# A guard of two columns becomes two guards of one column, a hand-written order of 745 operations replaces one of 725, and some casts change engine

## The chip, the cores and the metric

The kernel runs on one core of one Trainium2 chip. The metric is the device time of one execution in microseconds (us). Three runs of the kernel before gave 1259.17, 1256.1 and 1259.45 us; the median is 1259.17. The core's engines work side by side and wait for one another by semaphores: TensorE (PE, matrix products), VectorE (DVE), ScalarE (ACT), GpSimd (POOL) and SyncE (SP), whose queue here issues nearly all DMAs. Each engine carries out its own instructions in the order in which they were written.

## The reference, cut to what matters

An attention layer over 12288 tokens of 128 channels, with 768 keys made by pooling and one product, and then two feed-forward layers of width 2048:

```python
kv_pool = kv.reshape(B, H // r, r, W // r, r, C).mean(axis=(2, 4))
k = v = kv_pool.reshape(B, -1, C) @ w_sr
a = softmax(scale * (q @ k.T))
x = a @ v
h = x @ w_in
y = (maximum(h, 0) + alpha * minimum(h, 0)) @ w_out
h2 = y @ w_in2
out = (h2 * sigmoid(1.702 * h2)) @ w_out2
```

All inputs are float32 except the feed-forward weights, which come as 64-bit floats.

## The kernel before, in words

**Precision.** Nearly every product of float32 matrices is made as three float16 matmuls: each operand is split into a scaled high part and the rest (hi and lo), and hi·hi, lo·hi and hi·lo are summed in PSUM (`mm3`; lines 443 to 445 of the profile). Each split needs a power-of-two scale, which comes from the largest absolute value of the operand: `top_of` reduces each partition to its largest value (DVE), `total` (line 622) sums these over the partitions with a one-column matmul against a matrix of ones (called "scmm" here), and small DVE operations make the scale of the sum.

**The guard.** For tiles j > 2 the reduced values are raised to at least 2**-60 before `total`: one small DVE instruction, `max(a, 2**-60)`, called the guard. `x_prep(j)` prepares the attention's output x of tile j for the first feed-forward layer; for 2 < j < 22 it also prepares q of tile j+2, and there the two columns (column 0: x, column 1: q) go through one guard of 128x2, one scmm and one mask `scp`. In the profile the guard is `td<-ta` at line 408 (a helper's line), the scmm is `<-td,ones` at line 622.

**Tiles.** The tokens are cut into 24 tiles of 512. Of each tile there are four attention subtiles of 128 tokens (`att_tile`: product S, row maximum on DVE, exponential `exp` on ACT, normalised high part `ah` on ACT, low part `al` on DVE, and two DMA transposes `eh` and `el` issued by SP), six products with v (`att_v`), and 16 steps each of four feed-forward products: `l1`, `l2` with w1 and w2, `l3`, `l4` with w3 and w4. One step of l1 and of l3 needs two ACT operations (activation and high part), one DVE operation and a low part, mostly on POOL.

**Where the exponential goes.** For tiles 0 and 1 `exp` writes into an SBUF buffer `e` (two of them); for later tiles it writes back into PSUM, over S. The table `LO_ACT` says for which subtiles the low part is made on POOL, after a second scaled copy `es` on ACT.

**The start.** Twelve blocks of kv (512 KB each), q0 and q1 (256 KB each) and the eight weight blocks (1 MB each, "raw") are loaded over SP's queue. The pooled keys are twelve `kvmm` products; five of the blocks are first folded on DVE or POOL (`kvred`, table `KV_ON`). The weights are turned from 64-bit floats to pairs of float16 on chip (`conv`: per half matrix some 5 or 6 operations of 0.7 to 2.4 us on ACT, DVE and POOL; tables `CONV`, `HI_VEC`, `LO_VEC` choose the engine) after a reduction that finds their scale (`stats`).

**The order of the work.** `record` lists 6453 operations with a cost each, and `Plan.order` lays them out: first the operations whose numbers stand in the list `ORDER`, in that order (725 of them, up to about the second tile), then greedily by priority: at each step every engine's earliest ready operation is looked at, with the ends and latencies that the planner reckons. An operand may carry an offset, `(buffer, part, off)`: the planner then reckons it ready `off` ns earlier (a negative one: later). Offsets and costs change the order alone; the program's own waits are made by semaphores. Instructions are written in the order of the planned starts. [...] In gaps that the planner sees on PE between 20 and 60 us it puts dummy matmuls ("warm", line 1072).

What the steps below touch: `total` (616), `scale_of` (629), `att_tile` (around 686), `x_prep` (757), the tables from 323 on, and `ORDER` (86).

Of the kernel before, what the change touches and what calls it, by code (L numbers as in the profile page):

```python
# [16 lines left out]
AF = mybir.ActivationFunctionType  # L17
ALU = mybir.AluOpType
# [52 lines left out]
class Op:  # L71
# [14 lines left out]
ORDER = [3, 7, 8, 15, 9, 11, 10, 17, 16, 23, 13, 14, 20, 12, 18, 47, 171, 1, 2, 48, 49, 172, 41, 25, 26, 173, 4, 42, 27, 174, 50, 51, 175, 44, 52,  # L86
# [238 lines left out]
LO_ACT = [[1, 0, 1, 0], [0, 0, 0, 0]]  # L325
VEC = {'g1h': [0, 8384, 41304], 'g1l': [256, 128, 11032], 'g2h': [2560, 33322, 58609], 'g2l': [40298, 8194, 2884]}
GPS = {'g1': [0, 32896, 16], 'g2': [2688, 2, 20480]}
CONV = {'w10': 3, 'w11': 2, 'w20': 3, 'w21': 2, 'w30': 1, 'w31': 1, 'w40': 2, 'w41': 3}
LO_VEC = {'w10': 0, 'w11': 0, 'w20': 0, 'w21': 0, 'w30': 0, 'w31': 0, 'w40': 0, 'w41': 1}
HI_VEC = {'w10': 1, 'w11': 2, 'w20': 0, 'w21': 1, 'w30': 1, 'w31': 0, 'w40': 0, 'w41': 0}  # L330
# [53 lines left out]
def record(nc, T):  # L384

    pl = Plan()
    op = pl.op
# [11 lines left out]
    A = None if nc is None else nc.scalar  # L399
    G = None if nc is None else nc.gpsimd  # L400
# [11 lines left out]
    def small(fn, r, w, prio, gate=None, occ=66, dur=150, name="small", lock=False):  # L412
        return op("DVE", occ, dur, fn, r, w, prio, gate, name, lock)
# [22 lines left out]
    def new(name):  # L436
        return rings[name].buf(name)
# [178 lines left out]
    def total(pool, cols_, least, prio, n=1):  # L616

        pm = pool.buf("pt")

        def f():  # L620
            for i, (c, _) in enumerate(cols_):
                mm(out=pm.ap[:, 0:n], lhsT=T["ones"], rhs=c(), start=i == 0, stop=least is None and i == len(cols_) - 1)  # L622
            if least is not None:
                mm(out=pm.ap[:, 0:n], lhsT=T["ones"], rhs=least, start=False, stop=True)
        op("PE", 45 * len(cols_) + (45 if least is not None else 0), 0, f, [b for _, b in cols_] + [B["ones"]], [pm], prio, name="scmm")
        return pm

    def scale_of(d, pool, kc, kcb, prio, j=0):
        if j > 2:
            a, d = d, new("td")  # L630
            small(lambda: ts(d.ap, a.ap, 2.0 ** -60, ALU.max), [a], [d], prio)
        pm = total(pool, [(lambda: d.ap, d)], None if j > 2 else T["least"], prio)
# [48 lines left out]
    def att_tile(j, t, prio, gate):  # L681
# [23 lines left out]
        e = new("e") if j < 2 else s  # L705
        sm = new("sm")
        src = lambda: s.ap[:, :, 0:HALF]
        dst = (lambda: e.ap) if j < 2 else src
# [7 lines left out]
        op("ACT", 800, 905, lambda: A.activation(ah.ap, dst(), AF.Copy, scale=r.ap), [e, r], [ah], prio + 1.6, name=f"ah{j},{t}")  # L716
# [5 lines left out]
        if j < 2 and LO_ACT[j][t]:  # L722
# [7 lines left out]
        else:  # L730
            op("DVE", 933, 1019, lambda: V.scalar_tensor_tensor(out=al.ap, in0=dst(), scalar=r.ap, in1=ah.ap, op0=ALU.mult,  # L731
                                                                op1=ALU.subtract), [e, r, ah], [al], prio + 2.2, name=f"al{j},{t}",
               lock=j < 2)
# [25 lines left out]
    def x_prep(j, prio):  # L759
        x = xacc[j]  # L760
        pl.tag = f"X{j}"
        if 2 < j < NB - 2:
# [5 lines left out]
            small(lambda: ts(d.ap, a.ap, 2.0 ** -60, ALU.max), [(a, 0), (a, 1)], [d], prio + .01)  # L768
            pm = total(pool_h, [(lambda: d.ap, d)], None, prio + .1, 2)
# [346 lines left out]
```

## Time and profile before

| | us |
|---|---|
| median of three runs (lowest, highest) | 1259.17 (1256.1, 1259.45) |
| the profiled execution's own time | 1257.87 |
| its span in the trace | 1255.8 |
| PE busy in the span | 1215.5 (97%) |
| ACT busy | 1099.7 (88%) |
| DVE busy | 1005.0 (80%) |
| POOL busy | 804.8 (64%) |

The span is what the trace shows from the first instruction to the last; 2.1 us lie around it. "Busy" counts an engine's instructions, the dummy matmuls among PE's. Matmuls overlap: one of 512 columns is listed with 379 ns, and in a row of them the next starts after 215 ns.

### The profile page before, as it was taken

To read this page: it belongs to the slowest core of one execution; us is meant where nothing else is said; L and a number is where in the kernel's file an instruction comes from. 1 tells how busy PE (TensorE), PEld (TensorE's weight loads), DVE (VectorE), ACT (ScalarE), POOL (GpSimd) and SP (SyncE) were. 2 spreads that over 40 slices of the span, in tenths; PEclk is the share of its full clock that TensorE was granted. 3 is DMA by queue.
4 is the path that set the end of the run, shared out by engine and by line. 5 is a ranking of instruction groups with operands and counts; after the bars stand their busy time and mean duration, and the time that the engine had idled before them with its cause. 6 is when DMAs were issued, how large, how long until landed. Compare 5 with 4: busy or idle time off the path is not lost.

```text
span 1255.8 us, 18308 instructions
## 1 busy us (share of the span) xinstructions
PE 1215.5 (97%) x5829; PEld 569.3 (45%) x5832; DVE 1005.0 (80%) x1821; ACT 1099.7 (88%) x1939; POOL 804.8 (64%) x688
## 2 busy tenths in 40 slices
PE   5699999999999999999999999999999999999998
PEld 4344444444444444444444444444444444444443
DVE  5999998887877877878778778787787787876756
ACT  1899888888989989889899898898998988988888
POOL 1577566666657666666576666665766766667764
PEclk9999999999999999999999999999999999999999
DMA  9932222222121123121211221212111212120000
GB/s 372 215 62 48 44 43 47 53 37 46 35 55 35 36 45 55 34 47 34 56 34 38 43 55 34 46 36 55 34 40 41 55 34 47 34 47 13 9 10 17
DMA packets 165377, 66.67 MB, mean 53 GB/s; under 512 B 156448, under 2 KB 156576, under 8 KB 164256
## 3 DMA queue, kind: packets, MB, share of 16 engines
q1 hardware_dynamic: 164992, 65.43, 23.4%
q8 instruction: 45, 0.74, 0.2%
q14 instruction: 52, 0.43, 0.1%
q10 hardware_dynamic: 288, 0.07, 0.0%
HBM read 21.05 MB, written 6.29 MB: 22 GB/s over the span
## 4 chain that ended last, share of the span: by engine, by line
PE 60%; DVE 3%; ACT 1%; issue 0%; DMA 0%; POOLq 0%; POOL 0%; SPq 0%; ACTq 0%
PE bk L445 12%; PE bk L444 12%; PE bk L443 12%; PE hb L443 6%; PE hb L444 6%; PE hb L445 6%; PE sa L692 1%; PE sa L693 1%; PE sa L696 1%; DVE td L408 1%; DVE arena L832 1%; DVE ta L766 1%; ACT arena L808 0%; DMA q<-in_q 0%; PE hb L622 0%
## 5 line engine op out<-in xcount | busy, mean ns | idle before, releaser
L811 POOL TENSOR_TENSOR arena<-arena 128x512 f16<-128x512 f32 x656 | 769.0, 1191 | 403.4 <-ACT arena L808 286.9
L808 ACT CAST arena<-arena 128x512 f16<-128x512 f32 x740 | 449.5, 631 | 64.4 <-DVE arena L832 27.1
L873 DVE SCALAR_TENSOR_TENSOR arena<-arena,hb 128x512 f32<-128x512 f32 x261 | 178.8, 685 | 57.6 <-ACT arena L871 55.2
L832 DVE SCALAR_TENSOR_TENSOR arena<-arena,oma,hb 128x512 f32<-128x512 f32 x262 | 194.4, 743 | 29.9 <-ACT arena L830 26.3
L871 ACT ACTIVATE arena<-hb,yu 128x512 f32<-128x512 f32 x261 | 183.1, 702 | 12.8 <-PE hb L445 11.2
L830 ACT ACTIVATE arena<-hb 128x512 f32<-128x512 f32 x262 | 160.3, 613 | 23.1 <-PE hb L445 18.3
L445 PE MATMUL bk<-arena,w2h 128*128 128x512 f16 x384 | 145.6, 379 | 0.7 <-POOL arena L811 0.7
L445 PE MATMUL bk<-arena,w4h 128*128 128x512 f16 x384 | 145.6, 379 | 0.2 <-POOL arena L811 0.2
L444 PE MATMUL bk<-arena,w4l 128*128 128x512 f16 x384 | 145.6, 379 | 0.0
L443 PE MATMUL bk<-arena,w4h 128*128 128x512 f16 x384 | 145.6, 379 | 0.0
L444 PE MATMUL bk<-arena,w2l 128*128 128x512 f16 x384 | 145.6, 379 | 0.0
L443 PE MATMUL bk<-arena,w2h 128*128 128x512 f16 x384 | 145.6, 379 | 0.0
L873 DVE SCALAR_TENSOR_TENSOR arena<-arena,bk 128x512 f32<-128x512 f32 x123 | 84.1, 683 | 37.4 <-ACT arena L871 37.1
L731 DVE SCALAR_TENSOR_TENSOR alo<-sa,r,ah 128x768 f16<-128x768 f32 x88 | 89.5, 1017 | 18.1 <-ACT ah L716 13.0
L832 DVE SCALAR_TENSOR_TENSOR arena<-arena,oma,bk 128x512 f32<-128x512 f32 x122 | 90.7, 744 | 12.6 <-ACT arena L830 10.0
L443 PE MATMUL hb<-xh,w1h 128*128 128x512 f16 x262 | 99.2, 379 | 1.2 <-ACT xh L640 0.9
L443 PE MATMUL hb<-yh,w3h 128*128 128x512 f16 x261 | 98.9, 379 | 0.8 <-DVE arena L873 0.8
L445 PE MATMUL hb<-xl,w1h 128*128 128x512 f16 x262 | 99.3, 379 | 0.2 <-DVE xl L642 0.2
L444 PE MATMUL hb<-xh,w1l 128*128 128x512 f16 x262 | 99.3, 379 | 0.0
L445 PE MATMUL hb<-yl,w3h 128*128 128x512 f16 x261 | 98.9, 379 | 0.0
L444 PE MATMUL hb<-yh,w3l 128*128 128x512 f16 x261 | 98.9, 379 | 0.0
L871 ACT ACTIVATE arena<-bk,yu 128x512 f32<-128x512 f32 x123 | 85.3, 693 | 12.2 <-PE bk L445 10.6
(159 smaller groups left out, 2102.8 us busy)
## 6 DMA issues: line engine op xcount, KB each, us to landing
q<-in_q SPq DMA_DIRECT2D x24, 256.0 KB, 3.0
arena<-in_kv SPq DMA_DIRECT2D x12, 512.0 KB, 10.0
out<-arena SPq DMA_DIRECT2D x24, 256.0 KB, 2.0
raw<-in_moe_w_in SPq DMA_DIRECT2D x4, 1024.0 KB, 13.8
raw<-in_moe_w_out SPq DMA_DIRECT2D x4, 1024.0 KB, 12.0
eh<-ah SPq DMA_TRANSPOSE x96, 2.8
el<-alo SPq DMA_TRANSPOSE x96, 2.8
wsr<-in_w_sr ACTq DMA_DIRECT2D x1, 64.0 KB, 2.8
```

The lines of the kernel that those rows point to most:

```text
L408: return V.tensor_scalar(out=out, in0=in0, scalar1=s1, scalar2=None, op0=op0)
L443: mm(out=o, lhsT=wh, rhs=xh, start=start, stop=False)
L444: mm(out=o, lhsT=wl, rhs=xh, start=False, stop=False)
L445: mm(out=o, lhsT=wh, rhs=xl, start=False, stop=stop)
L692: mm(out=s.ap[:, h, 0:HALF], lhsT=qh[j].ap[:, ts_], rhs=T["k_hi"][:, hs], start=True, stop=False)
L731: op("DVE", 933, 1019, lambda: V.scalar_tensor_tensor(out=al.ap, in0=dst(), scalar=r.ap, in1=ah.ap, op0=ALU.mult, op1=ALU.subtract), [e, r ...
L808: op("ACT", act(508, n), act(618, n), lambda: A.copy(cols(hi.ap, j), cols(g.ap, j)), [g], [hi], s + 1.2, name=f"{nm}h{j},{m}")
L811: lambda: (V if on else G).tensor_tensor(out=cols(lo.ap, j), in0=cols(g.ap, j), in1=cols(hi.ap, j), op=ALU.subtract),
L830: op("ACT", act(488, n), act(597, n), lambda: A.activation(cols(g.ap, j), cols(h.ap, j), AF.Relu, scale=-1.0), [h], [g], s + .3, name=f"re ...
L832: op("DVE", dve(658, n), dve(746, n), lambda: V.scalar_tensor_tensor(out=cols(g.ap, j), in0=cols(g.ap, j), scalar=T["oma"][:, m:m + 1], in ...
L871: op("ACT", act(581, n), act(687, n), lambda: A.activation(cols(g.ap, j), cols(h.ap, j), AF.Tanh, scale=u.ap[:, 0:1]), [h, u], [g], s + .3 ...
L873: op("DVE", dve(605, n), dve(687, n), lambda: V.scalar_tensor_tensor(out=cols(g.ap, j), in0=cols(g.ap, j), scalar=1.0, in1=cols(h.ap, j), ...
```

## The change

The three parts of the code:

```diff
-    def total(pool, cols_, least, prio, n=1):
+    def total(pool, cols_, least, prio, n=1, need=None):
...
-        op("PE", 45 * len(cols_) + (45 if least is not None else 0), 0, f, [b for _, b in cols_] + [B["ones"]], [pm], prio, name="scmm")
+        op("PE", 45 * len(cols_) + (45 if least is not None else 0), 0, f, (need or [b for _, b in cols_]) + [B["ones"]], [pm], prio, name="scmm")
...
-        pm = total(pool, [(lambda: d.ap, d)], None if j > 2 else T["least"], prio)
+        pm = total(pool, [(lambda: d.ap, d)], None if j > 2 else T["least"], prio, 1, [(d, None, -300 if j > 2 else 0)])
...
-            small(lambda: ts(d.ap, a.ap, 2.0 ** -60, ALU.max), [(a, 0), (a, 1)], [d], prio + .01)
-            pm = total(pool_h, [(lambda: d.ap, d)], None, prio + .1, 2)
+            for k in (1, 0):
+                small(lambda k=k: ts(d.ap[:, k:k + 1], a.ap[:, k:k + 1], 2.0 ** -60, ALU.max), [(a, k)], [(d, k)], prio + .01)
+            pm = total(pool_h, [(lambda: d.ap, d)], None, prio + .1, 2, [(d, 0, -300), (d, 1, -300)])
```

So the guard of x_prep becomes two guards of 128x1, q's column first, and for j > 2 the planner reckons the scmm's operand ready 300 ns after the guard's end.

```diff
-LO_ACT = [[1, 0, 1, 0], [0, 0, 0, 0]]
-VEC = {'g1h': [0, 8384, 41304], 'g1l': [256, 128, 11032], 'g2h': [2560, 33322, 58609], 'g2l': [40298, 8194, 2884]}
-GPS = {'g1': [0, 32896, 16], 'g2': [2688, 2, 20480]}
-CONV = {'w10': 3, 'w11': 2, 'w20': 3, 'w21': 2, 'w30': 1, 'w31': 1, 'w40': 2, 'w41': 3}
-LO_VEC = {'w10': 0, 'w11': 0, 'w20': 0, 'w21': 0, 'w30': 0, 'w31': 0, 'w40': 0, 'w41': 1}
-HI_VEC = {'w10': 1, 'w11': 2, 'w20': 0, 'w21': 1, 'w30': 1, 'w31': 0, 'w40': 0, 'w41': 0}
+LO_ACT = [[1, 0, 1, 0], [0, 1, 0, 1], [0, 0, 0, 0], [0, 0, 0, 0]]
+HI_GPS = [[0, 0, 0, 0], [0, 0, 0, 0], [0, 0, 0, 0], [0, 0, 0, 0]]
+VEC = {'g1h': [0, 8384, 41904], 'g1l': [1280, 2216, 10936], 'g2h': [2560, 41642, 58545], 'g2l': [7530, 8210, 19140]}
+GPS = {'g1': [0, 32896, 32896], 'g2': [2692, 2, 32784]}
+CONV = {'w10': 1, 'w11': 2, 'w20': 3, 'w21': 2, 'w30': 1, 'w31': 1, 'w40': 2, 'w41': 3}
+LO_VEC = {'w10': 0, 'w11': 0, 'w20': 0, 'w21': 1, 'w30': 0, 'w31': 0, 'w40': 0, 'w41': 1}
+HI_VEC = {'w10': 0, 'w11': 2, 'w20': 2, 'w21': 1, 'w30': 2, 'w31': 0, 'w40': 0, 'w41': 0}
...
+        apart = j < len(HI_GPS)
-        e = new("e") if j < 2 else s
+        e = new("e") if apart else s
...
-               lock=j < 2)
+               lock=apart)
```

In words: the first weight block w10 has its low bits shifted out and its high half cast on ACT instead of DVE; the high half of w20 goes from ACT to POOL, that of w30 from DVE to POOL; the low half of w21 goes from POOL to DVE; subtiles 1 and 3 of tile 1 get an `es` on ACT and their `al` on POOL; `exp` of tiles 2 and 3 writes into the SBUF buffer `e`; and of the casts of the first three tiles some change engine (VEC: to DVE, GPS: high parts to POOL). `HI_GPS` is all zeros.

The list `ORDER` is new throughout (725 numbers become 745):

```diff
-ORDER = [3, 7, 8, 15, 9, 11, 10, 17, 16, 23, 13, 14, 20, 12, 18, 47, 171, 1, 2, 48, 49, 172, 41, 25, 26, 173, 4, 42, 27, 174, 50, 51, 175, 44, 52,
...
+ORDER = [3, 17, 11, 9, 8, 13, 12, 14, 21, 10, 7, 16, 20, 15, 23, 18, 1, 33, 2, 34, 171, 172, 173, 174, 25, 35, 0, 36, 37, 68, 38, 26, 67, 69, 39,
...
```

Read by engine and by name, what changes on SP and on PE up to the first steps of l1 (the small products of the weight scales are left out; `kv2` is a block of kv, `w31` a weight block, `eh0,2` the transpose of the high part of subtile 2 of tile 0, `V` the product with v, `X0:scmm` the scmm of x of tile 0):

```text
SP before: q0 kv4 kv1 kv0 q1 kv8 kv6 kv9 kv11 kv5 w10 kv10 w11 kv3 kv2 kv7 w20 w31 w30 w21 w41 vThi vTlo
           eh0,0 el0,2 eh0,2 el0,0 eh0,1 el0,1 eh0,3 el0,3 q2 w40 eh1,1 q3 el1,2 el1,1
SP after:  kv6 q1 kv0 kv4 kv5 w11 w10 kv7 kv8 q0 kv9 kv10 kv1 kv11 kv3 kv2 w20 q2 w21 w41 w30 vThi vTlo
           eh0,2 eh0,0 el0,2 el0,0 eh0,1 el0,1 eh0,3 el0,3 w31 eh1,1 el1,2 w40 el1,1 eh1,2 q3
PE before: Q0:scmm Q1:scmm kvmm20 kvmm00 (ten more kvmm) scmm S0,2 S0,0 S0,1 S0,3 S1,1 S1,2 V0,0 V0,1 V0,2 V0,3 S1,0
           X0:scmm Q2:scmm L1 0,3 L1 0,0 L1 0,1 S1,3 L1 0,5
PE after:  kvmm10 Q1:scmm kvmm11 kvmm12 (nine more kvmm, Q0:scmm among them) scmm Q2:scmm S0,2 S0,0 S0,1 S0,3 S1,1 V0,0 S1,2
           V0,1 V0,2 V0,3 S1,0 X0:scmm L1 0,2 S1,3 L1 0,0
```

On DVE, the reduction of q1 and the setting of the matrix of ones stand behind the fold of kv4 (`kvred10`) instead of ahead of everything; between the low parts `al0,1` and `al0,3` stands one weight reduction (`statw30`) instead of two conversion steps; the reduction of q2 is moved from the middle of x_prep of tile 0 to ahead of the first `klo`, and `max1,0` now stands inside that x_prep. On ACT, `es1,1` and `exp1,0` stand between the high part of x of tile 0 and the first `relu`, and the step of w40 that stood there comes later.

## Rows read from the trace of the kernel before

**Rows 1.** The page: busy us of each engine, its share of the span, instructions.
```profile
PE 1215.5 (97%) x5829; PEld 569.3 (45%) x5832; DVE 1005.0 (80%) x1821; ACT 1099.7 (88%) x1939; POOL 804.8 (64%) x688
```

**Rows 2.** Stages: length, then busy us of PE, PEld, DVE, ACT, POOL; clock, DMA share, GB/s.
```profile
11.57:32.30 20.73, 18.97 (x80) 14.81 (x82) 15.79 (x27) 4.96 (x8) 4.36 (x6) 1.00 1.02 419
32.30:48.00 15.70, 9.26 (x48) 4.56 (x49) 15.58 (x43) 12.65 (x19) 10.93 (x6) 1.00 1.00 227
...
400.00:500.00 100.00, 98.89 (x472) 45.68 (x471) 80.11 (x142) 90.52 (x162) 65.45 (x57) 1.00 0.22 43
```

**Rows 3.** Who waited for whom, TensorE: us in total, times, longest us.
```profile
PE hb L622 <- DVE td L408: 8.6, 17, 0.5
PE bk L622 <- DVE td L408: 1.0, 3, 0.5
```

**Rows 4.** Timeline 363 to 367 us: start, length, engine, line, operation.
```profile
364.02 1.15 POOL L811 TENSOR_TENSOR arena<-arena 128x512 f16<-128x512 f32 x1 [0.69 <-ACT arena L808]
364.10 1.10 DVE L408 TENSOR_SCALAR td<-ta 128x2 bf16<-128x2 f32 x1
...
364.36 0.38 PE L445 MATMUL bk<-arena,w2h 128*128 128x512 f16 x1
...
365.25 0.16 PE L622 MATMUL hb<-td,ones 128*128 128x2 bf16 x1 [0.51 <-DVE td L408]
```

**Rows 5.** Groups on VectorE by shape: count | busy us, mean ns | idle before.
```profile
L408 DVE TENSOR_SCALAR td<-ta 128x2 bf16<-128x2 f32 x19 | 19.6, 1032 | 0.0
...
L408 DVE TENSOR_SCALAR td<-ta 128x1 bf16<-128x1 f32 x25 | 3.7, 149 | 0.0
```

**Rows 6.** Timeline 329.5 to 335 us, around a guard of one column.
```profile
330.68 2.27 POOL L811 TENSOR_TENSOR arena<-arena 128x512 f16<-128x512 f32 x2 [0.27 <-ACT arena L808]
...
331.32 0.15 DVE L408 TENSOR_SCALAR td<-ta 128x1 bf16<-128x1 f32 x1
```

**Rows 7.** Timeline 311 to 319 us, from the scmm to the next tile.
```profile
317.30 0.75 DVE L642 SCALAR_TENSOR_TENSOR xl<-bk,scc,xh 128x512 f16<-128x512 f32 x1
...
318.66 0.38 PE L443 MATMUL bk<-xh,w1h 128*128 128x512 f16 x1
```

**Rows 8.** Timeline 0 to 62 us, VectorE: why TensorE begins late, and al0,3.
```profile
10.42 0.69 DVE L612 TENSOR_REDUCE td<-q 128x1 bf16<-128x512 f32 x1 [5.64 <-DMA q<-in_q]
...
15.54 1.97 DVE L515 TENSOR_REDUCE fold<-arena 128x256 f32<-128x1024 f32 x1 [1.37 <-DMA arena<-in_kv]
...
48.21 1.00 DVE L731 SCALAR_TENSOR_TENSOR alo<-e,r,ah 128x768 f16<-128x768 f32 x1
```

**Rows 9.** Timeline 0 to 62 us, TensorE.
```profile
11.57 0.19 PE L622 MATMUL bk<-td,ones 128*128 128x1 bf16 x1 [11.57 <-DVE least_v L453]
...
27.89 1.89 PE L509 MATMUL bk<-arena,wsr 128*128 128x256 f32 x8
...
52.51 0.22 PE L445 MATMUL bk<-el,v_hi 128*128 128x128 f16 x1 [0.30 <-DMA el<-alo]
...
53.40 0.33 PE L692 MATMUL sa<-k_hi,qh 128*128 128x384 f16 x1
...
56.16 0.38 PE L443 MATMUL hb<-xh,w1h 128*128 128x512 f16 x1 [0.89 <-ACT xh L640]
```

**Rows 10.** Timeline 0 to 110 us, SP's queue.
```profile
40.40 1.21 SPq L720 DMA_TRANSPOSE eh<-ah  x1
...
49.69 1.24 SPq L734 DMA_TRANSPOSE el<-alo  x1
```

**Rows 11.** Timeline 26 to 62 us, ScalarE.
```profile
50.83 0.97 ACT L709 ACTIVATE e<-sa,nm,qu 128x768 f32<-128x768 f32 x1
...
57.34 1.16 ACT L578 ACTIVATE raw<-raw 128x1024 int32<-128x1024 uint16 x1 [1.23 <-DMA raw<-in_moe_w_out]
```

**Rows 12.** Groups on VectorE by shape: low parts with one and with two SBUF inputs.
```profile
L642 DVE SCALAR_TENSOR_TENSOR yl<-yc,scc,yh 128x512 f16<-128x512 f32 x24 | 24.1, 1005 | 0.1
L642 DVE SCALAR_TENSOR_TENSOR xl<-bk,scc,xh 128x512 f16<-128x512 f32 x24 | 17.9, 744 | 0.0
```

More of the change, by code (lines that the diff above doesn't have):

```diff
@@ L704, in att_tile @@
         small(lambda: ts(nm.ap, nm.ap, qsc[j].ap, ALU.mult), [nm, qsc[j]], [nm], prio + .61, occ=130, dur=214)
-        e = new("e") if j < 2 else s
+        apart = j < len(HI_GPS)
+        e = new("e") if apart else s
         sm = new("sm")
         src = lambda: s.ap[:, :, 0:HALF]
-        dst = (lambda: e.ap) if j < 2 else src
+        dst = (lambda: e.ap) if apart else src
         op("ACT", 890, 985, lambda: A.activation(dst(), src(), AF.Exp, bias=nm.ap, scale=qsc[j].ap, accum_out=sm.ap),
@@ L715, in att_tile @@
         ah, al = new("ah"), new("alo")
-        op("ACT", 800, 905, lambda: A.activation(ah.ap, dst(), AF.Copy, scale=r.ap), [e, r], [ah], prio + 1.6, name=f"ah{j},{t}")
+        if apart and HI_GPS[j][t]:
+            op("POOL", 820, 860, lambda: G.tensor_scalar(out=ah.ap, in0=e.ap, scalar1=r.ap, scalar2=None, op0=ALU.mult), [e, r], [ah],
+               prio + 1.6, name=f"ah{j},{t}")
+        else:
+            op("ACT", 800, 905, lambda: A.activation(ah.ap, dst(), AF.Copy, scale=r.ap), [e, r], [ah], prio + 1.6, name=f"ah{j},{t}")
         if t == 0:
@@ L721, in att_tile @@
            [ah], [(eh[j], t)], prio + 2, name=f"eh{j},{t}")
-        if j < 2 and LO_ACT[j][t]:
+        if apart and LO_ACT[j][t]:
             if LO_ACT[j][t] == 1:
```

51 rows, old and new, of the table ORDER are left out of this document.

## The prediction, made before the changed kernel ran

> **What bounds the kernel now.** I read the page first. TensorE is busy for 97% of the span; the next, ScalarE, for 88% [rows 1]. So time is lost only where TensorE idles or does dummy work, 40.3 us of the span (1255.8 less 1215.5), and I looked for that by stage. In the steady part 100 us hold 98.89 us of TensorE work [rows 2]: 1.11 us are missing. In the start TensorE begins only at 11.57, is nearly full until 32.30, and then works 9.26 of 15.70 us [rows 2].
>
> The waits say what is missing in the steady part. TensorE waited 17 times, 8.6 us in all, at a scmm for its guard; three more such waits make 1.0 us [rows 3]. The timeline shows one: the guard of two columns starts at 364.10 and takes 1.10 us, so it ends at 365.20, and the scmm starts at 365.25 after 0.51 us of idle TensorE [rows 4]. The same instruction with one column takes 149 ns, the one with two columns 1032 ns on average [rows 5]. What holds it is seen in the same rows: a GpSimd subtraction runs from 364.02 to 365.17, and the guard ends 0.03 us behind it [rows 4]. A guard of one column that starts inside a GpSimd operation (330.68 to 332.95) takes 0.15 us [rows 6]. So the guard of two columns waits for GpSimd, and that of one column does not.
>
> **The sum, part by part**, against the profiled execution's own time, 1257.87 us. That lies 1.3 us below the median of the three runs and inside their spread, so I add nothing for it.
>
> *Guard split, and scmm reckoned 300 ns later.* Removed: 19 guards of 1.03 us. Added: 38 of 0.15 us, in all 5.7 us where there were 19.6, on an engine that is 80 us busy in 100 [rows 5, 2]; their cost is nothing, since VectorE gets time back. Started at 364.10, the guard of x would end at 364.25. The matmul ahead of the scmm starts at 364.36 [rows 4], so TensorE is not free for the scmm before about 364.58, and the wait of 0.51 us goes wholly. What is late next? The scmm's result makes the scale, then xh and xl. xl is done at 318.05 and the next tile's first matmul starts at 318.66 [rows 7]: 0.6 us to spare, and the chain itself comes earlier. The planner's 300 ns only lets it put another matmul ahead of the scmm. Nothing queues behind that wait which isn't there today. Gain: 8.6 us; ends 8.0 (0.03 us left at each) and 9.6 (the other 1.0 us too).
>
> [...]
>
> *Loads in a new order.* Ahead of the last kv block the queue carries the same in both orders: twelve blocks, q0, q1, w10 and w11, 8.9 MB, at 419 GB/s [rows 2] some 21 us. The reduction of q1 no longer holds up TensorE's start: now it waits until 10.42 for q1 [rows 8], and TensorE behind it to 11.57 [rows 9]. But the new first product waits for a fold of 1.97 us [rows 8] of the fourth block. The last block's product starts at 27.89 [rows 9], when transfers end either way. I take 0; ends 0.6 us earlier and 1.8 later (one product of 1.89 us, rows 9, caught behind the last block).
>
> *Transposes of tile 0.* Eight follow each other from 40.40 to 49.69, 1.33 us apart [rows 10]; SP is their bound, and it begins with subtile 0 although subtile 2 is ready before. The last lands for the product at 52.51 [rows 9]. The new order begins with subtile 2, and the last low part (48.21 now, rows 8) stands behind one weight reduction instead of two conversions. But X0's scmm stands behind S1,0, which needs exp1,2, and that ends on ScalarE at 51.80 [rows 11], where its place is much the same. S1,0 starts at 53.40 now, behind the product that waited for that transpose [rows 9]: so at most 1.6 us of the way to the first l1 step (56.16, rows 9) can go, and max1,0 over 768 columns, now inside that x_prep in place of q2's reduction over 512 (0.69 by its like, rows 8), takes some 0.3 back. I take 1.3 us gained; ends 2.0 gained and 1.0 lost.
>
> *First steps of l1.* ScalarE's wait of 1.23 us for w40, ahead of the first relu, goes [rows 11]; es1,1, a ScalarE pass over 768 columns, shorter than the exponential of 0.97 [rows 11], takes its place, and w31 is now asked for only after the last transpose of tile 0. I take 0.3 gained; ends 1.5 gained and 2.0 lost.
>
> *Casts and low parts on other engines.* Single operations of about 1 us, from or to a GpSimd that is busy 64% [rows 1]; ScalarE's and VectorE's shares in the start change by about two operations each. GpSimd's idle third is the cover: I take 0. If it is gone in the start, one operation late on the path is 1 to 2 us, which is within the ends of the first steps.
>
> *Exponential of tiles 2 and 3 in SBUF.* Eight low parts get two SBUF inputs in place of one. The like pair in the trace takes 1005 ns with two and 744 with one [rows 12]: 0.26 us each, 2.1 us on VectorE. I take 0.3 us on TensorE's path; ends 0 and 2.1.
>
> Sum: 1257.87 - 8.6 - 0 - 1.3 - 0.3 + 0 + 0.3 = **1248.0 us**, the start giving 1.3.
>
> **Rivals.** (1) *A late transfer costs the start 3.5 us or more.* Instructions wait in written order, so one late block (w31 on VectorE ahead of the first prelu, or q2 ahead of klo) holds the whole chain. For it: the order before was held up by just that, twice (5.64 us for q1, rows 8; 1.23 for w40, rows 11). Against: w31 is asked for earlier than w40 was. Time: 1257.87 - 8.6 + 3.5 = 1252.8.
>
> (2) *The low parts of tiles 2 and 3 are blocked outright.* A VectorE instruction that reads two SBUF tensors would wait for a whole GpSimd operation, 1.15 us [rows 4], eight times: 9.2 us where I reckon 0.3, all on TensorE's path: 1248.0 + 8.9 = 1256.9, no change. For it: the 0.26 us above. Against: 0.26 is not 1.15, and VectorE has slack. [...]
>
> (3) *The change doesn't remove the wait*: the guard is held by something that also holds one column. Then 1257.87 - 1.3 = 1256.6. Against: 25 guards of one column, 149 ns on average [rows 5].
>
> (4) *Slower: the next tile's first l1 step waits for xl.* The scmm is planned 300 ns later, and if the greedy order then puts several products ahead of it, xl is late at each of some 20 tiles. It decides once xl comes over 0.6 us later than now against that step [rows 7]. To end 3.8 us above today it must take back 8.6 + 1.3 + 3.8 = 13.7 us, 0.7 us a tile, so xl would be 1.3 us later than now: 1261.7. Against: 300 ns are less than what the guard gives back (0.9).
>
> **How the numbers follow.** 0.3% or 3.8 us, about what a measurement can tell, is 1255.4. Chances: forecast 0.74 (faster); rival 1 0.14 (0.11 faster, 0.03 same, by how late); rival 2 0.04 and rival 3 0.04 (same); rival 4 0.04 (slower). Faster 0.85, same 0.11, slower 0.04. The range: the gains' ends together give 1257.87 - 9.6 - 4.1 = 1244.2, and the lowest run lies 1.8 below the profiled one: 1242.5. Upwards it takes in rival 1 with a little over: 1253.5. Rivals 2 to 4 lie outside, 0.12 in all.
>
> **What would show each step.** Right: no wait of scmm for the guard in the list of waits, guards of one column at 0.15 us, 100 us of the steady part with over 99.7 us of TensorE, tiles 0.5 us shorter each; the first l1 step before 55.5 us; the low parts of tiles 2 and 3 at about 1.0 to 1.3 us. Wrong: a steady part with a new releaser ahead of an l1 or l3 matmul; a DMA as releaser of VectorE or ScalarE between 30 and 60 us; TensorE's busy time in the first 65 us no higher than now without the dummies.

## The result, and the profile after

| | before | after |
|---|---|---|
| median us (lowest, highest) | 1258.58 (1256.1, 1259.45), 4 runs | 1242.07 (1241.7, 1243.21), 4 runs |
| the profiled execution's own time | 1257.87 | 1243.21 |
| its span in the trace | 1255.8 | 1241.4 |

The ratio is 0.9876, with a 95% interval of 0.9861 to 0.9892: some 16.5 us faster between the medians, 14.4 us between the two spans. The forecast was 1248.0. What follows explains the 14.4 us of the spans, where each microsecond can be found. The profiled execution of the changed kernel is the longest of its four, 1.1 us above their median.

The page after, busy us of each engine (it answers to rows 1):

```profile
PE 1214.1 (98%) x5833; PEld 570.7 (46%) x5833; DVE 992.7 (80%) x1842; ACT 1101.0 (89%) x1940; POOL 803.7 (65%) x687
```

TensorE's busy time is 1.4 us less than before in a span that is 14.4 us shorter. Next, who waited for whom on TensorE, after (us in total, times, longest us), and the guard among the groups by shape:

```profile
PE bk L524 <- DVE fold L517: 10.6, 2, 10.5
PE sa L694 <- ACT e L712: 4.3, 4, 2.1
PE hb L445 <- DVE arena L840: 1.9, 2, 1.5
PE bk L538 <- DVE r L715: 1.5, 1, 1.5
```

```profile
L410 DVE TENSOR_SCALAR td<-ta 128x1 bf16<-128x1 f32 x63 | 9.4, 149 | 0.0
```

The wait of the scmm for the guard [rows 3] is nowhere in the list, and all 63 guards have one column and 149 ns [rows 5]. The longest entry is TensorE's start, once. So the wait went as forecast. How much it was worth is read from one stretch that begins and ends at the same instruction: the scmm of x, from one tile to the sixteenth after it. These rows come from the view of busy time by stretch, the first of the kernel before, the second and third after (length, then PE, PEld, DVE, ACT, POOL; granted clock; DMA share; GB/s):

```profile
264.94:1067.77 802.83, 794.04 (x3777) 366.74 (x3777) 644.27 (x1136) 725.61 (x1297) 526.40 (x448) 1.00 0.21 43
```

```profile
264.63:1054.18 789.55, 789.55 (x3777) 366.72 (x3776) 630.91 (x1153) 724.86 (x1297) 526.60 (x448) 1.00 0.22 43
...
400.00:500.00 100.00, 100.00 (x480) 46.47 (x479) 80.04 (x147) 91.31 (x164) 66.01 (x57) 1.00 0.22 43
```

The same 3777 matmuls take 13.28 us less, 0.83 us for each of the 16 tiles (50.18 to 49.35 us). TensorE's idle time in the stretch, 802.83 - 794.04 = 8.79 us, is gone; but its *busy* time fell too, by 4.49 us, with the same matmuls. So a third of the gain had stood in the profile as work. At the first end of the stretch the new kernel is only 0.3 us ahead (264.63 against 264.94), and behind the second 0.8 us more are gained (14.4 less 13.6). Part of that 0.8 belongs ahead of the stretch, because the scmm stands three matmuls (0.65 us) later in the new order: by the first l1 product of tile 5 the new kernel is 0.96 us ahead (270.16 against 271.12). Three of the guards lie before that product. By the first l1 product of tile 3 the new kernel is still 0.45 us behind (173.79 against 173.34). So 13.3 us come from the sixteen tiles, and the start itself gave nothing.

**The start.** TensorE at its beginning, and around the first l1 step, after (start, length, engine, line, operation); of the first l1 step's rows, those that set its time:

```profile
10.49 1.22 PE L524 MATMUL bk<-fold,wsr 128*128 128x256 f32 x2 [10.49 <-DVE fold L517]
...
26.18 1.91 PE L511 MATMUL bk<-arena,wsr 128*128 128x256 f32 x8
27.93 0.59 PE L524 MATMUL bk<-fold,wsr 128*128 128x256 f32 x2
...
29.14 1.02 PE L1080 MATMUL sbk<-warm 128*128 128x512 bf16 x4
...
31.13 0.16 PE L624 MATMUL bk<-td,ones 128*128 128x1 bf16 x1 [0.97 <-DVE k_lo L910]
...
31.18 0.32 PE L694 MATMUL sa<-k_hi,qh 128*128 128x384 f16 x1
...
41.06 1.64 POOL L735 TENSOR_TENSOR alo<-e,ah 128x768 f16<-128x768 f32 x1 [0.15 <-ACT e L731]
41.22 1.51 DVE L412 TENSOR_SCALAR oma<-al 128x16 f32<-128x16 f32 x1
...
54.58 0.69 DVE L614 TENSOR_REDUCE td<-bk 128x1 bf16<-128x512 f32 x1 [0.34 <-PE bk L447]
...
57.66 0.38 PE L445 MATMUL hb<-xh,w1h 128*128 128x512 f16 x1 [0.80 <-ACT xh L642]
```

The attention's first product S comes at 31.18, 1.12 us ahead of 32.30 [rows 2]: the last product on the pooled keys is now that of a folded block (0.59 us at 27.93), where an unfolded one of 1.89 us stood at 27.89 [rows 9]. But this is no gain of the new order. Four kernels below keep the old order (the first three experiments and the sixth), and their first S comes at 31.24, 31.21, 31.01 and 31.15; here the third of them:

```profile
31.01 0.32 PE L692 MATMUL sa<-k_hi,qh 128*128 128x384 f16 x1 [0.57 <-ACT k_hi L901]
```

In that profile the reduction of q1 begins at 9.00 instead of 10.42 [rows 8], so the loads came earlier with the old order as well; why they differ between executions is open. The first l1 step comes at 57.66, 1.50 us *behind* 56.16 [rows 9]. Two rows show trouble between. oma, the setting of 1 - alpha (128x16), takes 1.51 us, and ends 0.03 us behind the GpSimd operation beside it (41.06 + 1.64): it is held as the two-column guard was in rows 4. And the granted clock falls below 1.00: matmuls of 384 columns that are listed with 0.32 us and start 0.16 apart at 35.53 are listed with 0.53 and start 0.32 apart at 32.85. By stretches of 5 us, after:

```profile
30.00:35.00 5.00, 4.01 (x16) 1.85 (x15) 3.52 (x11) 2.44 (x5) 2.72 (x2) 0.68 1.00 415
...
45.00:50.00 5.00, 2.32 (x21) 1.60 (x21) 4.96 (x8) 4.69 (x8) 0.00 (x0) 0.89 0.61 117
50.00:55.00 5.00, 5.00 (x61) 4.43 (x60) 3.82 (x12) 3.63 (x5) 1.98 (x2) 0.77 0.88 246
```

In the kernel before the clock was 1.00 in all three; the middle one there:

```profile
45.00:50.00 5.00, 2.25 (x27) 1.66 (x26) 5.00 (x10) 5.00 (x7) 0.14 (x1) 1.00 0.76 143
```

Ahead of the first fall TensorE had done four dummy matmuls (29.14 to 30.16) and then waited 0.97 us for VectorE's low part of the keys; ahead of the last it had worked 2.32 us of 5. The kernel before had worked no more there (2.25), so these rows do not say why the clock fell in the one and not in the other. oma and the clock are two suspects for the start; both are tried below.

### The profile page after: what moved, and what is told of

It is laid out like the page before. It is cut to its first block, busy times and chain, and to the rows that moved or that the text cites. A ratio compares the mean times of both kernels' runs of the same rounds, so it can differ in the third digit from the quotient of the medians.

```text
span 1241.4 us, 18330 instructions
## 1 busy us (share of the span) xinstructions
PE 1214.1 (98%) x5833; PEld 570.7 (46%) x5833; DVE 992.7 (80%) x1842; ACT 1101.0 (89%) x1940; POOL 803.7 (65%) x687
## 4 chain that ended last, share of the span: by engine, by line
PE 91%; DVE 2%; ACT 2%; issue 1%; POOLq 0%; POOL 0%; ACTq 0%
PE bk L445 20%; PE bk L447 20%; PE bk L446 20%; PE hb L445 9%; PE hb L447 9%; PE hb L446 9%; PE sa L694 2%; PE sa L695 2%; PE sa L698 2%; DVE arena L840 1%; ACT arena L838 0%; ACT arena L816 0%; DVE nm L704 0%; ACT e L712 0%; ACT ah L723 0%
## 5 line engine op out<-in xcount | busy, mean ns | idle before, releaser
L881 DVE SCALAR_TENSOR_TENSOR arena<-arena,hb 128x512 f32<-128x512 f32 x257 | 175.6, 684 | 69.2 <-ACT arena L879 67.3
L840 DVE SCALAR_TENSOR_TENSOR arena<-arena,oma,hb 128x512 f32<-128x512 f32 x255 | 188.8, 742 | 25.4 <-ACT arena L838 21.0
L879 ACT ACTIVATE arena<-hb,yu 128x512 f32<-128x512 f32 x257 | 179.5, 699 | 13.2 <-PE hb L447 10.3
L838 ACT ACTIVATE arena<-hb 128x512 f32<-128x512 f32 x255 | 155.2, 610 | 10.1 <-PE hb L447 4.6
L881 DVE SCALAR_TENSOR_TENSOR arena<-arena,bk 128x512 f32<-128x512 f32 x127 | 86.9, 684 | 37.0 <-ACT arena L879 36.2
L840 DVE SCALAR_TENSOR_TENSOR arena<-arena,oma,bk 128x512 f32<-128x512 f32 x129 | 95.8, 742 | 12.4 <-ACT arena L838 10.2
L447 PE MATMUL hb<-xl,w1h 128*128 128x512 f16 x255 | 96.6, 379 | 0.3 <-DVE bw L412 0.3
L819 DVE TENSOR_TENSOR arena<-arena 128x512 f16<-128x512 f32 x118 | 91.5, 779 | 5.4 <-ACT arena L816 2.2
L738 DVE SCALAR_TENSOR_TENSOR alo<-sa,r,ah 128x768 f16<-128x768 f32 x80 | 81.3, 1017 | 16.4 <-ACT ah L723 11.8
```

What stands on the lines that cost most here:

```text
L447: mm(out=o, lhsT=wh, rhs=xl, start=False, stop=stop)
L819: lambda: (V if on else G).tensor_tensor(out=cols(lo.ap, j), in0=cols(g.ap, j), in1=cols(hi.ap, j), op=ALU.subtract),
L838: op("ACT", act(488, n), act(597, n), lambda: A.activation(cols(g.ap, j), cols(h.ap, j), AF.Relu, scale=-1.0), [h], [g], s + .3, name=f"re ...
L840: op("DVE", dve(658, n), dve(746, n), lambda: V.scalar_tensor_tensor(out=cols(g.ap, j), in0=cols(g.ap, j), scalar=T["oma"][:, m:m + 1], in ...
L879: op("ACT", act(581, n), act(687, n), lambda: A.activation(cols(g.ap, j), cols(h.ap, j), AF.Tanh, scale=u.ap[:, 0:1]), [h, u], [g], s + .3 ...
L881: op("DVE", dve(605, n), dve(687, n), lambda: V.scalar_tensor_tensor(out=cols(g.ap, j), in0=cols(g.ap, j), scalar=1.0, in1=cols(h.ap, j), ...
```

## The experiments

Two theories of the gain were set against each other: that all of it is the scmm's waits, those that the profile counts as busy included; or that the forecast 8.6 us are the waits and the rest is the new order and tables. The first four kernels divide the change. Each is timed beside the kernel before on one chip, in three rounds: the first four kernels, the next four, the last two. The kernel before gave 1257.36, 1256.9 and 1257.29 us in these, and 1258.58 beside the changed kernel; so about a microsecond between the times of different rounds is not clear of noise.

**The split alone.** The kernel before, with this (`total` gets its argument `need`, here and below, which does nothing by itself):

```diff
-            small(lambda: ts(d.ap, a.ap, 2.0 ** -60, ALU.max), [(a, 0), (a, 1)], [d], prio + .01)
-            pm = total(pool_h, [(lambda: d.ap, d)], None, prio + .1, 2)
+            for k in (1, 0):
+                small(lambda k=k: ts(d.ap[:, k:k + 1], a.ap[:, k:k + 1], 2.0 ** -60, ALU.max), [(a, k)], [(d, k)], prio + .01)
+            pm = total(pool_h, [(lambda: d.ap, d)], None, prio + .1, 2, [(d, 0, 0), (d, 1, 0)])
```

> The kernel before with the guard split in two, and nothing else (no 300 ns, old order, old tables). Theory 1 (all of the gain per tile is scmm waiting for its guard; the profile's 0.51 us of idle leaves out 0.16 us, because the matmul ahead is listed as busy for 379 ns where the next could start after 215): the tile's period falls from 50.18 us by 0.68 to 49.51, and the time by 11 to 12 us. Theory 2 (the idle of 0.51 us is all that the guard cost, the rest of the 0.83 us per tile comes from the new order and tables): period 49.67, time 8.6 us less.

Measured: 1245.48 us (1244.81 to 1246.38) against 1257.36, ratio 0.9905 (0.9892 to 0.9919), 11.9 us. From 262.82 to 1055.10 sixteen tiles take 49.52 us each, 0.66 less than before.

**The 300 ns alone.** The guard keeps its two columns; only the planner's reckoning changes:

```diff
-        pm = total(pool, [(lambda: d.ap, d)], None if j > 2 else T["least"], prio)
+        pm = total(pool, [(lambda: d.ap, d)], None if j > 2 else T["least"], prio, 1, [(d, None, -300 if j > 2 else 0)])
...
-            pm = total(pool_h, [(lambda: d.ap, d)], None, prio + .1, 2)
+            pm = total(pool_h, [(lambda: d.ap, d)], None, prio + .1, 2, [(d, None, -300)])
```

> The kernel before with the 300 ns alone: the guard keeps its two columns, but for j > 2 the planner reckons every scmm's operand ready 300 ns after its guard. Theory 1: the scmm of y, which starts 0.41 us after the matmul ahead of it instead of 0.215, loses its hidden wait of 0.2 us; the scmm of x is moved behind at least one more triple of matmuls (0.65 us), which covers most of its 0.68 us: period 49.35 to 49.6, time 10 to 14 us less. Theory 2: the guard still waits for GpSimd, so at most 5 us less.

Measured: 1245.76 us (1245.43 to 1246.46), ratio 0.9908 (0.9894 to 0.9921), 11.6 us; 49.47 us a tile. So the 300 ns gain almost as much as the split, and *without* curing the guard. The groups by shape, and the timeline around one scmm of x, of this kernel:

```profile
L408 DVE TENSOR_SCALAR td<-ta 128x2 bf16<-128x2 f32 x19 | 19.5, 1025 | 0.0
```

```profile
313.12 2.46 POOL L811 TENSOR_TENSOR arena<-arena 128x512 f16<-128x512 f32 x2 [0.26 <-PE hb L445]
...
313.46 0.85 DVE L408 TENSOR_SCALAR td<-ta 128x2 bf16<-128x2 f32 x1
313.59 0.38 PE L443 MATMUL hb<-xh,w1h 128*128 128x512 f16 x1
313.80 0.38 PE L444 MATMUL hb<-xh,w1l 128*128 128x512 f16 x1
314.02 0.38 PE L445 MATMUL hb<-xl,w1h 128*128 128x512 f16 x1
314.36 0.16 PE L622 MATMUL bk<-td,ones 128*128 128x2 bf16 x1
```

The guard still takes about a microsecond, but a whole l1 step of three matmuls now stands ahead of the scmm (in rows 4 the scmm came straight behind the l2 step). Its last matmul starts at 314.02 and the scmm at 314.36: 0.34 us where 0.215 is the pitch, so 0.12 us are still lost, and the view lists no idle time for them.

**Both, with the old order and tables.** The kernel before, with:

```diff
+        pm = total(pool, [(lambda: d.ap, d)], None if j > 2 else T["least"], prio, 1, [(d, None, -300 if j > 2 else 0)])
...
+            for k in (1, 0):
+                small(lambda k=k: ts(d.ap[:, k:k + 1], a.ap[:, k:k + 1], 2.0 ** -60, ALU.max), [(a, k)], [(d, k)], prio + .01)
+            pm = total(pool_h, [(lambda: d.ap, d)], None, prio + .1, 2, [(d, 0, -300), (d, 1, -300)])
```

> The kernel before with the split and the 300 ns, but the old order and the old tables. Theory 1: period 49.35 as in the changed kernel, time 13 to 14.5 us less, so within 2 us of the changed kernel. Theory 2: period 49.67, time 8.6 us less, so 5 to 6 us above the changed kernel.

Measured: 1242.75 us (1241.9 to 1243.21), ratio 0.9881 (0.9866 to 0.9896), 14.6 us; 49.36 us a tile. That is the changed kernel's time within 0.7 us.

**The new order and tables alone.** The changed kernel, with the guard of two columns and no 300 ns (one number of `ORDER` follows, since a guard less is counted):

```diff
-        pm = total(pool, [(lambda: d.ap, d)], None if j > 2 else T["least"], prio, 1, [(d, None, -300 if j > 2 else 0)])
+        pm = total(pool, [(lambda: d.ap, d)], None if j > 2 else T["least"], prio)
...
-            for k in (1, 0):
...
+            small(lambda: ts(d.ap, a.ap, 2.0 ** -60, ALU.max), [(a, 0), (a, 1)], [d], prio + .01)
+            pm = total(pool_h, [(lambda: d.ap, d)], None, prio + .1, 2)
```

> The changed kernel with the old guard of two columns and without the 300 ns: new order and new tables alone. Theory 1: period 50.18 or near it, time within 2 us of the kernel before. Theory 2: period 49.86, time 5 to 6 us less.

Measured: 1256.75 us (1255.52 to 1258.08, 11 runs) against 1257.36, ratio 0.9995 (0.9986 to 1.0004): no change. TensorE's waits in its profile:

```profile
PE bk L624 <- DVE td L410: 4.9, 9, 0.9
PE hb L624 <- DVE td L410: 4.5, 9, 0.7
```

The waits of rows 3 stand where they stood, 9.4 us (9.6 before). So the first theory holds: the gain is the scmm's waits, to within the 1.8 us that the interval leaves to order and tables. Where the part that the profile calls busy sits is seen in the timeline of the kernel *before*, around the scmm of y, in the stretch of rows 6:

```profile
331.11 0.38 PE L445 MATMUL bk<-arena,w4h 128*128 128x512 f16 x1
...
331.52 0.16 PE L622 MATMUL bk<-td,ones 128*128 128x1 bf16 x1
331.55 0.38 PE L443 MATMUL hb<-yh,w3h 128*128 128x512 f16 x1
```

and after, around y's scmm and then around x's:

```profile
329.95 0.38 PE L447 MATMUL hb<-yl,w3h 128*128 128x512 f16 x1
330.17 0.17 PE L624 MATMUL bk<-td,ones 128*128 128x1 bf16 x1
...
313.15 2.31 POOL L819 TENSOR_TENSOR arena<-arena 128x512 f16<-128x512 f32 x2 [0.26 <-ACT arena L816]
...
313.48 0.15 DVE L410 TENSOR_SCALAR td<-ta 128x1 bf16<-128x1 f32 x1
...
313.72 0.38 PE L447 MATMUL bk<-xl,w1h 128*128 128x512 f16 x1
313.94 0.17 PE L624 MATMUL hb<-td,ones 128*128 128x2 bf16 x1
```

After, both start 0.22 us behind the start of the matmul ahead. Before, y's scmm starts 0.41 us behind the start of the matmul ahead of it, after 0.22 us. The pitch in a row of them is 0.215. So TensorE stood still for 0.195 us, but the matmul ahead is listed with 0.38 us, which covers the gap up to 0.03 us. The same holds at x: in rows 4 the scmm starts 0.89 us behind the matmul ahead, so 0.675 us were lost, of which the list shows 0.51. Together 0.87 us a tile by these two rows; the split takes 0.66 of it, the 300 ns 0.71, both 0.82.

**The changed kernel without the 300 ns.**

```diff
-        pm = total(pool, [(lambda: d.ap, d)], None if j > 2 else T["least"], prio, 1, [(d, None, -300 if j > 2 else 0)])
+        pm = total(pool, [(lambda: d.ap, d)], None if j > 2 else T["least"], prio)
...
-            pm = total(pool_h, [(lambda: d.ap, d)], None, prio + .1, 2, [(d, 0, -300), (d, 1, -300)])
+            pm = total(pool_h, [(lambda: d.ap, d)], None, prio + .1, 2, [(d, 0, 0), (d, 1, 0)])
```

> The changed kernel without the 300 ns: split, new order and new tables stay. Theory 1 (split worth 0.68 us a tile, 300 ns worth another 0.2 by the scmm of y): period 49.5 us, 2.5 to 3.5 us above the changed kernel. If with the new order the scmm of x also comes too early for its guard, up to 6 us above. If the 300 ns do nothing here, no difference.

Measured: 1245.28 us (1243.97 to 1245.59) against 1256.9, ratio 0.9904 (0.9889 to 0.9918); 49.54 us a tile. That is 3.2 us behind the changed kernel, and in the old order it was 2.7: the 300 ns are worth about the same in either.

This kernel and the split alone differ in order and tables only. The first l1 step comes at 56.45 here and at 55.00 there, 1.45 us earlier in the old order. Yet the first l1 product of tile 5 starts at the same time in both, first the split alone, then this kernel:

```profile
269.00 0.38 PE L443 MATMUL hb<-xh,w1h 128*128 128x512 f16 x1
...
269.00 0.38 PE L445 MATMUL bk<-xh,w1h 128*128 128x512 f16 x1
```

The times agree too (1245.48 and 1245.28). So a later first l1 step need not reach the end of the kernel.

**A guard of two columns by another instruction.** What is it in the guard that GpSimd holds: two columns, or the operation? The kernel before, with the guard made by a reduction over pairs, one of each pair a constant 2**-60 written once:

```diff
...
-            small(lambda: ts(d.ap, a.ap, 2.0 ** -60, ALU.max), [(a, 0), (a, 1)], [d], prio + .01)
+            small(lambda: V.tensor_reduce(out=d.ap, in_=a.ap, axis=AX.X, op=ALU.max), [(a, 0), (a, 1)], [d], prio + .01)
```

> The kernel before with one guard still, of two columns in one instruction, but made by a reduction over pairs (the value beside a constant 2**-60) in place of the tensor_scalar. [...] If two columns as such, or the wait for two writers, make it wait: 1.0 us a guard and no gain.

Measured: 1245.7 us (1245.55 to 1246.08), ratio 0.9909 (0.9895 to 0.9924), 49.55 us a tile, as with the split. Groups by shape:

```profile
L408 DVE TENSOR_SCALAR td<-ta 128x1 bf16<-128x1 f32 x25 | 3.7, 148 | 0.0
...
L772 DVE TENSOR_REDUCE td<-ta 128x2 bf16<-128x4 f32 x19 | 2.8, 149 | 0.0
```

The reduction writes two columns in 149 ns, where TENSOR_SCALAR took 1032 [rows 5]. One of them starts at 312.71, inside two GpSimd operations in a row (312.38 to 314.68), and takes 0.15 us. So it is the operation together with its shape: the TENSOR_SCALAR with two columns in SBUF waits for GpSimd (each of the 19 in the kernel before starts inside a GpSimd operation, and 18 of them end 0.01 to 0.04 us behind it), with one column it doesn't (149 ns), and a reduction with two doesn't (149 ns). Why the two-column form is held and the other two are not is not shown.

**More dummy matmuls in the start.** The first of the two suspects there. The changed kernel, with dummies also in smaller gaps (47 in place of 22):

```diff
-                while t - free[e] > 1000 + 216 * clock.at(free[e]):
+                while t - free[e] > 300 + 216 * clock.at(free[e]):
```

> The changed kernel with dummy matmuls on TensorE from planned gaps of 0.5 us on instead of 1.2 (47 of them in place of 22). Theory A (the new order's start is given back because TensorE falls to its lower clock at 31.7 us and at 48.9 us): granted clock 1.00 throughout the start, S0,2 and S0,0 take 1.0 us each instead of 1.6 and 1.9, first l1 step 1 to 2 us earlier, time 1 to 2 us less. Theory B (the start is paced by ScalarE and VectorE, whatever TensorE's clock): time within 0.5 us.

Measured: 1240.51 us (1240.23 to 1240.62), ratio 0.9868 (0.9851 to 0.9884), 1.6 us faster than the changed kernel's median; between two rounds that is little, and the ratios' intervals overlap (0.9876 there). The clock and the first l1 step, of this kernel:

```profile
45.00:50.00 5.00, 3.52 (x44) 2.69 (x43) 4.97 (x9) 4.84 (x6) 1.04 (x1) 1.00 0.63 118
50.00:55.00 5.00, 4.96 (x42) 2.88 (x40) 4.83 (x14) 4.17 (x7) 2.37 (x2) 1.00 0.70 220
```

```profile
39.78 1.32 DVE L412 TENSOR_SCALAR oma<-al 128x16 f32<-128x16 f32 x1
...
51.67 0.67 DVE L614 TENSOR_REDUCE td<-bk 128x1 bf16<-128x512 f32 x1
...
54.59 0.38 PE L445 MATMUL hb<-xh,w1h 128*128 128x512 f16 x1
```

The clock is 1.00 in every stretch of 5 us from 30 to 60, x of tile 0 is reduced 2.9 us earlier (51.67 against 54.58) and the first l1 step comes 3.1 us earlier, against the slowest of the changed kernel's executions. oma is still held.

**oma earlier.** The second suspect. The changed kernel, with the operation moved ahead in `ORDER`, to behind the scale of the keys (and reckoned by the planner as ready, so that nothing else moves for it):

```diff
-... 57, 62, 283, 161, ... 152, 100, 102, 103, 108, 153, 5, 90, ...
+... 57, 62, 5, 283, 161, ... 152, 100, 102, 103, 108, 153, 90, ...
...
-    small(lambda: ts(T["oma"], T["al"], -1.0, ALU.mult, 1.0, ALU.add), [B["al"]], [B["oma"]], -990)
+    small(lambda: ts(T["oma"], T["al"], -1.0, ALU.mult, 1.0, ALU.add), [(B["al"], None, 20000)], [B["oma"]], -990)
```

> The changed kernel with one small VectorE operation of the start moved: 1 - alpha over 16 columns, which takes 1.51 us at 41.22 beside a GpSimd subtraction (0.28 in the kernel before), now stands behind kq at 31.4 us, where GpSimd idles. If an operation held by GpSimd costs there what it takes: al0,1 and ah0,1 0.8 to 1.2 us earlier, first l1 step up to 1 us earlier, time 0.5 to 1 us less. If the start is paced elsewhere: within 0.5 us.

Measured: 1240.89 us (1239.99 to 1241.12), ratio 0.9869 (0.9855 to 0.9884). oma takes 0.16 us, the first l1 step comes at 54.09. But in this profile the clock was 1.00 as well, without more dummies, so one run does not divide the two.

**Both**, and against it **the old order with the same dummies**: the last kernel and that of the third experiment, each with

```diff
-                while t - free[e] > 1000 + 216 * clock.at(free[e]):
+                while t - free[e] > 300 + 216 * clock.at(free[e]):
```

Of both start edits together:

> The changed kernel with both start edits: dummies in gaps over 300 ns, and the 1 - alpha operation (oma) moved behind the scmm chain of k. If the two repair different losses (the clock in the start, 1.6 us; oma held beside GpSimd, 0.5 us at the first l1 step with the clock held in both), the time is about 1240.0 and the first l1 step comes before 54.2 us. If the earlier oma gained only because its profile happened to keep the clock, it is no faster than the dummies alone: 1240.5, first l1 at 54.6.

Measured: 1239.61 us (1239.54 to 1240.47) against 1257.29, ratio 0.9861 (0.9845 to 0.9878); first l1 step at 53.72. This is the fastest kernel of the study, 2.5 us ahead of the changed kernel's median of another round. Against the dummies alone (clock 1.00 in both) the earlier oma brings the first l1 step from 54.59 to 53.72, 0.87 us, and the median from 1240.51 to 1239.61, though their single runs overlap. So by the first l1 step the two losses are separate ones, as the first expectation had it; the times agree, but do not prove it.

Of the old order with dummies:

> The old order and tables, guard split and 300 ns, and dummies in gaps over 300 ns. Theory that the new order is the better one once the clock is held: the old order's profiles show a clock of 1.00 in the start already, so the dummies give it nothing, 1242.75 within 0.5, first l1 step at about 56.1, 2 to 3 us behind the changed kernel with the same edits. Rival, that the two orders are worth the same and the dummies gain in each: 1240.5 to 1241.

Measured: 1243.87 us (1243.56 to 1244.2), ratio 0.9893 (0.9878 to 0.9908). Timeline of this kernel:

```profile
53.35 0.69 DVE L612 TENSOR_REDUCE td<-bk 128x1 bf16<-128x512 f32 x1 [0.33 <-PE bk L445]
...
54.84 0.69 DVE L612 TENSOR_REDUCE td<-q 128x1 bf16<-128x512 f32 x1 [0.79 <-DMA q<-in_q]
...
56.67 0.38 PE L443 MATMUL hb<-xh,w1h 128*128 128x512 f16 x1
```

The rival, 1240.5 to 1241, is out. With the clock at 1.00 in both, the first l1 step comes at 56.67 in the old order and at 54.59 in the new one, and the times are 1243.87 and 1240.51. So with this edit the new order is 3.4 us faster; without it, 0.7 (1242.75 against 1242.07). That this is what the order is worth is not shown. Of the 2.08 us at the first l1 step 1.24 are there at the first S already, old order first:

```profile
32.16 0.33 PE L692 MATMUL sa<-k_hi,qh 128*128 128x384 f16 x1
...
30.92 0.32 PE L694 MATMUL sa<-k_hi,qh 128*128 128x384 f16 x1
```

In four other profiles of the old order the first S came at 31.01 to 31.24. In this kernel the reduction of q2, in the middle of x_prep, waits 0.79 us for its transfer, and x of tile 0 is reduced 1.7 us later (53.35 against 51.67). That the dummies make the old order 1.1 us slower than without them (another round, and the intervals overlap) I had not expected, and whether it is so and why is open: without them, in the profile of the third experiment, the reduction of q2 did not wait and the first l1 step came at 55.84, although the clock was 0.66 there from 45 to 50 us. So the premise, that the old order's profiles show 1.00 already, was wrong: three of the five without more dummies show a fall (0.66 in the first experiment, from 40 to 45 us, 0.66 in the third and 0.68 in the sixth).

## Why the prediction was right or wrong

**The guard: the mechanism was right, the size was not.** The forecast said 8.6 us, ends 8.0 to 9.6; sixteen tiles alone gave 13.3. Two sentences of that step failed. "The wait of 0.51 us goes wholly" took the profile's idle time as the price of the wait; it begins at the listed end of the matmul ahead (0.38 us), while TensorE could have gone on after 0.215, so each wait was 0.16 us dearer. The forecast had the number beside it: TensorE free from 364.58, the scmm at 365.25 [rows 4], 0.67 us. By 19 waits of 0.675 us in place of 17 of 0.51 the term would have been 12.8. And "The planner's 300 ns only lets it put another matmul ahead of the scmm" priced at nothing what was worth as much as the split by itself: alone 11.6 us of gain, on top of the split 2.7. It moves the scmm of x behind work that is ready, and it closes a wait at y of 0.2 us a tile that no list shows. Nothing of this was out of reach: the start times in rows 4 give the 0.89, and the timeline of rows 6 the 0.41. That xl has "0.6 us to spare" held: no l1 step waits for xl in the steady part, which has TensorE at 100.00 of 100 us, though a wait under 0.16 us would not be listed there.

**Loads: 0 taken, and no run shows more.** The first S at 31.18 lies within what the old order gives in other profiles (31.01 to 31.24); the 1.12 us against the kernel before belong to its profiled execution, in which the loads came late.

**Transposes of tile 0 and first steps of l1: 1.3 and 0.3 us taken, 1.5 us lost in the profiled execution.** The sign named for it, the first l1 step before 55.5 us, did not come (57.66), nor in the two other profiles of the new order without an edit of the start (57.18 and 56.45); the old order without more dummies has 54.96 to 56.16. With the clock held it does come (54.59, and 53.72 with oma moved). What the step left out is the granted clock: it read 1.00 in the stages of rows 2 and carried every duration over, while in the start of the changed kernel it fell to 0.68, 0.89 and 0.77 in three stretches, with matmuls of 0.33 us listed at 0.53. Nor did the step see oma, which is no part of the diff and became 1.51 us because the new order set it near the beginning of a GpSimd operation (in the kernel before it stood at the end of one and took 0.28); with the clock held in both, moving it brings the first l1 step 0.87 us earlier. How the 1.5 us divide between the clock and oma in the changed kernel's own execution is not shown. They also did not last: order and tables alone change the time by nothing that can be measured (ratio 0.9995), so the start, forecast at 1.3 us of gain, gave none that shows.

**Casts, exponential of tiles 2 and 3: 0 and 0.3 taken, nothing seen.** The groups by shape, after, of low parts with the product in PSUM and in SBUF, and of y's:

```profile
L738 DVE SCALAR_TENSOR_TENSOR alo<-sa,r,ah 128x768 f16<-128x768 f32 x80 | 81.3, 1017 | 16.4 <-ACT ah L723 11.8
...
L644 DVE SCALAR_TENSOR_TENSOR yl<-yc,scc,yh 128x512 f16<-128x512 f32 x24 | 24.5, 1019 | 0.5 <-ACT yh L642 0.5
...
L738 DVE SCALAR_TENSOR_TENSOR alo<-e,r,ah 128x768 f16<-128x768 f32 x12 | 12.3, 1025 | 0.1
```

**The rivals.** (1) A late transfer in the start: not seen; no wait of VectorE or ScalarE for a transfer is listed between 30 and 60 us, and up to tile 3 the start lost 0.45 us, neither 3.5 lost nor 1.3 gained. (2) Low parts of tiles 2 and 3 blocked by GpSimd: false, 1025 ns with two SBUF inputs against 1017 with one. (3) The guard not cured: false, 149 ns. (4) xl late: false, as above. The median lies 0.4 us below the range's low end, 1242.5 (1242.4 by its own terms), because the ends of the guard's term were made from the same listed idle time as its middle. That it lies so near is luck: the low end holds 4.1 us of gains in the start, and none came.

**The second guard** costs 149 ns a tile on VectorE, and nothing that shows on TensorE's path, since the split alone gains 0.66 us a tile.

## What to carry to other kernels

Price a wait by start times: start of the waiting matmul less start of the one ahead, less the pitch in a full row; the listed idle time leaves out what the listed duration covers, and waits shorter than that are in no list at all (0.2 us a tile at y). Where a planner orders the work, letting it reckon the result of a short operation later, so that ready work is set ahead of the matmul that waits, can be worth as much as making the operation shorter. And before carrying the durations of a sparse stage into a new order, ask what the granted clock will be there (0.68 in one stretch of this start, 1.00 before), and which small operations come to stand beside GpSimd (oma: 1.51 us, 0.28 before).

## What the runs showed of the hardware that was not expected

- The guard as a TENSOR_SCALAR over 128x2 in SBUF was held until the GpSimd operation beside it ended (1032 ns on average; 18 of 19 ended 0.01 to 0.04 us behind it). Over 128x1 it was not (149), nor was a TENSOR_REDUCE that writes 128x2 (149). oma, a TENSOR_SCALAR over 128x16, ended 0.03 us behind the GpSimd operation as well (1.51 us, against 0.16 when it stood beside none).
- The granted clock in the start was 0.68 to 0.89 in three stretches of 5 us of the changed kernel, with matmuls of 0.33 us listed at 0.53, and 1.00 in all of them with 25 more dummy matmuls, with which the first l1 step came 3.1 us earlier. It was 1.00 too in the one profile with oma moved and no more dummies. The fall is not bound to one order: the old one showed it in three profiles (0.66, 0.66, 0.68).
